# Fetching and converting two early feed-forward weights at other steps of an attention loop

## The chip, the core and the metric

The kernel runs on one core of a Trainium2 chip. The metric is the device time of one execution in microseconds (us), start to end. TensorE (PE; its weight loads are listed as PEld), VectorE (DVE), ScalarE (ACT), GpSimd (POOL) and SyncE (SP) each take their own instructions in order; transfers are issued from a queue of SP, ACT or POOL and run on 16 DMA engines.

## The reference

Attention with a mixing of heads before and after the softmax, then two feed-forward blocks one after the other:

```python
scores = scale * np.matmul(q, k.transpose(0, 1, 3, 2))      # 2 x 12 heads x 448 x 448
scores = np.einsum('bhij,hg->bgij', scores, w_pre)
attn = softmax(scores)                                      # over j, with 1e-9 added to the sum
attn = np.einsum('bgij,gh->bhij', attn, w_post)
x = np.matmul(attn, v)                                      # as 896 x 768
x = (silu(x @ w_gate) * (x @ w_val)) @ w_out                # 768 -> 1536 -> 768
h = x @ w_in                                                # 768 -> 2048
out = (h * np.clip(h + 3, 0, 6) / 6) @ w_out2               # 2048 -> 768
```

The feed-forward weights arrive as 64-bit floats. Each is brought to 32 bits on the chip by one ACT and four DVE operations (`convert_w`), and then split into a high and a low part, since each product is made of three matmuls.

## The kernel before

The 896 rows of queries are cut into eight tiles of about 112, each with ten or so chunks; two chunks make one step. There are 45 steps (0 to 44), which a Python loop writes out in full (L617 to L663), with LOOK = 2 steps of look-ahead. In step i the program writes, in this order:

- `exps(i+1)` (L261): ACT's exponentials of the next step;
- `av` and `av_rest` (L318, L337): products of finished weights of an earlier tile with v, and `postmix(i)` (L287), 56 small matmuls that mix heads after the softmax;
- `attn_out(i)` (L306): DVE and ACT each copy one PSUM bank of `postmix` out; `weights(i+1)` (L269 to L273): DVE's reciprocals and scaled mixing weights `wn`;
- `premix(i+2)` (L239) and `row_max(i+2)` (L252): the mixing before the softmax and DVE's row maxima `nm`;
- `qk` (L171): scores of a later tile, copied to the SBUF tile S one step on by DVE and ACT (L187);
- `relayout` (L204): up to three transfers from S into `sx` on SP's queue, which `premix` reads later, the first of them behind this step's `postmix`; `relayout_rest` (L220) does the remaining rows on POOL's queue;
- at the step's end ("end"), whatever the table put there: loads of q, k and v, `fetch` (L479) and `convert` (L490).

From step 36 on all tiles are scored, so steps have no `qk` and are shorter.

The table works as follows. `fetch(j, "early")` issues a third of weight j (two of six 128-row blocks, 256 KB of 64-bit words, tile `rg` for the gate weight, j = 0, and `rv` for the value weight, j = 1) on SP's queue. `convert(j, part)` issues the next one or two of 15 conversion operations; every group of four steps handles one third: ACT's Abs together with DVE's clamp, then a shift, and two merges (L414 to L419). The early raw tile has one buffer, so the first fetch of weight 1 comes after the last conversion of weight 0. `halve` (L497) splits the two finished weights at steps 42 and 43, and their first products run between the last steps of attention. The rest of the program, from about 185 us on, is feed-forward work.

In the transfers' names `q` is a tile's queries, `sx` the relaid scores, and in the trace's groups a buffer's number is left out.

Of the kernel before, what the change touches and what calls it, by code (L numbers as in the profile page):

```python
# [48 lines left out]
def kernel(  # L49
# [493 lines left out]
    def at_step(i, f, *args, place="end"):  # L543
        extra[i][place].append((f, args))
# [50 lines left out]
        at_step(scored[4 * b + 3] + 1, new_x, b)  # L595
    loads = [(0, load_v, 0, 2), (1, load_v, 0, 3), (4, load_q, 3), (6, load_q, 4)]
    loads += [(7 + n, load_k, 1, n, n + 1) for n in range(HP)]
    loads += [(15, load_q, 5), (21, load_q, 6), (27, load_q, 7)]
    loads += [(20 + 2 * j, load_v, 1, j) for j in range(JC)]
    loads += [(n, fetch, 0, "early") for n in (14, 17, 19)] + [(n, fetch, 1, "early") for n in (30, 32, 34)]  # L600
    for i, *load in loads:
        at_step(i, *load)

    for j in range(2):
        for n in range(12):
            at_step(17 + 14 * j + n, convert, j, 2 if n % 4 == 0 else 1)

    fillers = None

# [216 lines left out]
```

## Time and profile before

| what | us |
|---|---|
| median of 3 runs | 676.01 |
| lowest, highest | 674.33, 677.24 |
| the profiled execution | 674.53 |
| its span, first to last instruction | 672.7 |
| PE busy in it | 660.0 |

All numbers of the trace come from the one profiled execution, which lies 1.48 us below the median. Where a step is named by its time, it runs from the row maximum (L252) of the step before to its own. The granted TensorE clock is 1.00 in all windows listed.

### The profile page before, as it was taken

To read this page: it belongs to the slowest core of one execution; us is meant where nothing else is said; L and a number is where in the kernel's file an instruction comes from. 1 tells how busy PE (TensorE), PEld (TensorE's weight loads), DVE (VectorE), ACT (ScalarE), POOL (GpSimd) and SP (SyncE) were. 2 spreads that over 40 slices of the span, in tenths; PEclk is the share of its full clock that TensorE was granted. 3 is DMA by queue.
4 is the path that set the end of the run, shared out by engine and by line. 5 is a ranking of instruction groups with operands and counts; after the bars stand their busy time and mean duration, and the time that the engine had idled before them with its cause. 6 is when DMAs were issued, how large, how long until landed. Compare 5 with 4: busy or idle time off the path is not lost.

```text
span 672.7 us, 16147 instructions
## 1 busy us (share of the span) xinstructions
PE 660.0 (98%) x6685; PEld 561.9 (84%) x6685; DVE 500.1 (74%) x836; ACT 296.8 (44%) x603; POOL 160.5 (24%) x204
## 2 busy tenths in 40 slices
PE   9899999899999999999999999999999999999997
PEld 3456666566899999999999999999999999999997
DVE  4877889789278888888787666668888888756550
ACT  4766777677243434343442323245444553332220
POOL 3543366545202111311111000013333332000000
PEclk9999999999999999999999999999999999999999
DMA  7776576445022323223242333313222333544420
GB/s 245 228 217 190 175 219 200 156 148 205 3 95 95 134 100 138 98 104 131 98 137 95 99 136 101 133 67 121 95 95 95 102 117 92 165 140 149 151 67 27
DMA packets 34937, 86.87 MB, mean 129 GB/s; under 512 B 10064, under 2 KB 22752, under 8 KB 34864
## 3 DMA queue, kind: packets, MB, share of 16 engines
q1 hardware_dynamic: 26208, 81.14, 36.5%
q0 software_dynamic: 7936, 3.94, 2.4%
q8 instruction: 52, 0.85, 0.5%
q10 hardware_dynamic: 720, 0.76, 0.3%
q14 instruction: 21, 0.17, 0.1%
HBM read 62.37 MB, written 2.75 MB: 97 GB/s over the span
## 4 chain that ended last, share of the span: by engine, by line
PE 76%; DVE 17%; ACT 3%; DMA 2%; issue 1%; SPq 0%; ACTq 0%
PE pp L441 15%; PE po L441 13%; PE pv L441 12%; PE pg L441 12%; DVE yi L490 9%; PE pqk L171 5%; PE ppost L287 5%; PE pav L318 5%; PE ppre L239 5%; DVE rl L714 2%; PE p L441 2%; PE pav L337 2%; DVE yp L490 2%; DVE li L432 2%; ACT hi L427 2%; DMA q<-in_q_dram 1%
## 5 line engine op out<-in xcount | busy, mean ns | idle before, releaser
L441 PE MATMUL pp<-g,hp 128*128 128x448 f32 x384 | 108.3, 363 | 0.0
L690 POOL TENSOR_TENSOR g<-rl,g 128x448 fp32r<-128x448 f32 x32 | 41.3, 1309 | 167.8 <-ACT g L689 167.8
L441 PE MATMUL po<-u,ho 128*128 128x448 f32 x288 | 80.7, 361 | 0.0
L441 PEld LDWEIGHTS pp<-g,hp 128*128 128x128 f32 x384 | 72.0, 188 | 4.8
L261 ACT ACTIVATE e<-ppre,nm 128x448 f32<-128x448 f32 x90 | 56.3, 631 | 32.6 <-DVE nm L252 32.5
L441 PE MATMUL pi<-x2h,li 128*128 128x448 f32 x192 | 69.7, 363 | 0.0
L441 PE MATMUL pi<-x2l,hi 128*128 128x448 f32 x192 | 69.6, 362 | 0.0
L441 PE MATMUL pp<-g,lp 128*128 128x448 f32 x192 | 69.3, 361 | 0.2 <-DVE lp L432 0.2
L441 PE MATMUL pi<-x2h,hi 128*128 128x448 f32 x192 | 69.1, 360 | 0.0
L690 POOL TENSOR_TENSOR u<-sg,u 128x448 fp32r<-128x448 f32 x24 | 32.6, 1377 | 149.6 <-ACT u L689 149.6
L220 POOL DMA_DIRECT2D sx<-S x90 | 52.4, 583 | 50.8 <-issue 16.4
L441 PEld LDWEIGHTS po<-u,ho 128*128 128x128 f32 x288 | 54.0, 187 | 4.1
L287 PE MATMUL ppost<-wn,e 60*64 60x60 f32 x2520 | 51.3, 220 | 4.9 <-DVE wn L273 2.6
L252 DVE TENSOR_REDUCE nm<-ppre 128x1 f32<-128x448 f32 x90 | 51.8, 617 | 4.6 <-PE ppre L239 1.9
L441 PE MATMUL po<-u,lo 128*128 128x448 f32 x144 | 52.3, 363 | 0.0
L287 PEld LDWEIGHTS ppost<-wn,e 60*64 60x64 f32 x2520 | 45.2, 134 | 8.2 <-ACT at L306 3.0
L318 PEld LDWEIGHTS pav<-at,v 128*64 128x64 f32 x576 | 28.0, 136 | 28.7 <-ACT xs L360 15.7
L171 PE MATMUL pqk<-k,q 64*64 64x448 f32 (+3 forms) x384 | 48.1, 540 | 1.7 <-DMA q<-in_q_dram 1.4
L441 PE MATMUL pg<-xh,lg 128*128 128x448 f32 x132 | 47.9, 363 | 0.0
L441 PE MATMUL pv<-xh,lv 128*128 128x448 f32 x132 | 47.9, 363 | 0.0
L441 PE MATMUL pv<-xl,hv 128*128 128x448 f32 x132 | 47.8, 362 | 0.0
L441 PE MATMUL pg<-xl,hg 128*128 128x448 f32 x132 | 47.8, 362 | 0.0
(98 smaller groups left out, 1401.0 us busy)
## 6 DMA issues: line engine op xcount, KB each, us to landing
sx<-S SPq DMA_DIRECT2D x90, 182.0 KB
ri<-in_moe_w_in_dram SPq DMA_DIRECT2D x16, 768.0 KB
ro<-in_moe_w_out_dram SPq DMA_DIRECT2D x12, 768.0 KB
rg<-in_moe_w_gate_dram SPq DMA_DIRECT2D x11, 768.0 KB
rv<-in_moe_w_val_dram SPq DMA_DIRECT2D x11, 768.0 KB
rp<-in_moe_w_out_dram SPq DMA_DIRECT2D x12, 640.0 KB
rp<-in_moe_w_out_dram SPq DMA_DIRECT2D x6, 768.0 KB
sx<-S POOLq DMA_DIRECT2D x90, 42.0 KB, 4.7
```

The lines of the kernel that those rows point to most:

```text
L171: nc.tensor.matmul(p[e][lo:hi, :S], lhsT=qs[t][r, base + lo : base + hi], rhs=ks[b][r, c, :], start=True, stop=True, tile_position=(64 * e ...
L220: nc.gpsimd.dma_start(out=sx[m // 2][104:128, m % 2, :], in_=rows)
L239: nc.tensor.matmul(p[a][64 * r : 64 * r + 64, :S], lhsT=W1[rows, :], rhs=x[rows, r, :], start=True, stop=True, tile_position=(64 * a, 64 * r),
L252: top = nc.vector.tensor_reduce(nm[:, a : a + 1], pre[i][a][:, :S], AX.X, ALU.max, negate=True)
L261: nc.scalar.activation(e2[a], p[a][:, :S], AF.Exp, bias=nm[:, a : a + 1], scale=1.0, accum_out=sm[:, a : a + 1])
L287: mm = nc.tensor.matmul(p[s][64 * c : 64 * c + 64, at, :, :], lhsT=e2[a][rows, 64 * k : 64 * k + 64], rhs=wn[rows, a, :].rearrange("p (g k ...
L318: nc.tensor.matmul(p[64 * e : 64 * e + 64, : 2 * n], lhsT=vs[b][:, jc, h, :], rhs=ats[t][:, 2 * jc : 2 * jc + 2, h, :n], start=jc == 0, st ...
L337: mm = nc.tensor.matmul(pavs[t, c][64 * e : 64 * e + 64, a * n : a * n + n], lhsT=vs[b][rows, JC - 1, h, :], rhs=ats[t][rows, KB - 1, h, : ...
L427: nc.scalar.copy(hi_flat, y)
L441: nc.tensor.matmul(p[:, :S], lhsT=wt[:, kk, :], rhs=xx, start=start, stop=stop)
L490: f(*args)
L690: eng.tensor_tensor(to[1], src, to[0].bitcast(F32), ALU.subtract)
```

## The change

Three lines of the table are changed. The fetches of weight 0 go from the ends of steps 14, 17 and 19 to those of 13, 14 and 16, those of weight 1 from 30, 32 and 34 to 27, 29 and 31. The conversions of weight 0 go from steps 17 to 28 to steps 15 to 26, those of weight 1 from 31 to 42 to 28 to 39. The load of the last tile's q goes from the end of step 27 to that of step 28. It is read first by `qk` in step 30.

```diff
-    loads += [(15, load_q, 5), (21, load_q, 6), (27, load_q, 7)]
+    loads += [(15, load_q, 5), (21, load_q, 6), (28, load_q, 7)]
     loads += [(20 + 2 * j, load_v, 1, j) for j in range(JC)]
-    loads += [(n, fetch, 0, "early") for n in (14, 17, 19)] + [(n, fetch, 1, "early") for n in (30, 32, 34)]
+    loads += [(n, fetch, 0, "early") for n in (13, 14, 16)] + [(n, fetch, 1, "early") for n in (27, 29, 31)]
...
     for j in range(2):
         for n in range(12):
-            at_step(17 + 14 * j + n, convert, j, 2 if n % 4 == 0 else 1)
+            at_step(15 + 13 * j + n, convert, j, 2 if n % 4 == 0 else 1)
```

No instruction is added or dropped, and PE's and POOL's orders are the same. On SP's queue, around the ends of steps 27 to 31 (`S_119` and `S_120` are the two score tiles), there stands before:

```order
L204 DMA sx_2404<-S_120 104x1x448
L111 DMA q_2407<-in_q_dram 128x708
L204 DMA sx_2404<-S_120 104x1x448
L204 DMA sx_2485<-S_120 104x1x448
L204 DMA sx_2485<-S_119 104x1x448
L479 DMA rv_0_2633<-in_moe_w_val_dram 128x256
L204 DMA sx_2635<-S_119 104x1x448 x2
```

and after:

```order
L204 DMA sx_2406<-S_120 104x1x448
L479 DMA rv_0_2409<-in_moe_w_val_dram 128x256
L204 DMA sx_2406<-S_120 104x1x448
L204 DMA sx_2486<-S_120 104x1x448
L111 DMA q_2488<-in_q_dram 128x708
L479 DMA rv_0_2409<-in_moe_w_val_dram 128x256
L204 DMA sx_2486<-S_119 104x1x448
L204 DMA sx_2641<-S_119 104x1x448 x2
```

The first third of `rv` stands where q stood; q and the second third stand ahead of the transfer from `S_119`, where nothing but relayouts stood.

On ACT, at the end of step 28 (`xs` is the copy that closes it, the two `e` are the exponentials of step 29), there stands before:

```order
L306 COPY at_2467<-ppost_1_2430 128x84x5
L360 COPY xs_2072<-pav_5_2419 128x108
L261 ACTIVATE e_123,sm_2489<-ppre_0_2470,nm_2476 128x448
L261 ACTIVATE e_124,sm_2489<-ppre_1_2471,nm_2476 128x448
L187 COPY S_119<-pqk_4_1_2480 119x448
```

and after:

```order
L306 COPY at_2468<-ppost_1_2431 128x84x5
L360 COPY xs_2074<-pav_5_2420 128x108
L490 ACTIVATE yv_0_2490<-rv_0_2409 128x256
L261 ACTIVATE e_123,sm_2494<-ppre_0_2471,nm_2477 128x448
L261 ACTIVATE e_124,sm_2494<-ppre_1_2472,nm_2477 128x448
L187 COPY S_119<-pqk_4_1_2481 119x448
```

The first Abs of the value weight now stands ahead of the exponentials written in step 29.

On DVE, in steps 40 and 41, there stands before:

```order
L252 TENSOR_REDUCE nm_3376<-ppre_1_3371 128x1
L490 TENSOR_SCALAR yv_0_2715<-yv_0_2715 128x256
L348 MEMSET turns 1x1
L306 COPY at_3361<-ppost_0_3393 128x84x5
L269 TENSOR_SCALAR rc_3427<-sm_3380 128x2
L270 RECIPROCAL rc_3427<-rc_3427 128x2
L273 TENSOR_TENSOR wn_3430<-W_110,rc_3427 128x120
L382 TENSOR_TENSOR xl_3095<-pav_0_3383,xh_3094 128x110
L252 TENSOR_REDUCE nm_3440<-ppre_0_3434 128x1
L252 TENSOR_REDUCE nm_3440<-ppre_1_3435 128x1
L490 SCALAR_TENSOR_TENSOR yv_0_2715<-rv_0_2633,yv_0_2715 128x256
```

and after:

```order
L252 TENSOR_REDUCE nm_3379<-ppre_1_3374 128x1
L348 MEMSET turns 1x1
L306 COPY at_3364<-ppost_0_3395 128x84x5
L269 TENSOR_SCALAR rc_3429<-sm_3382 128x2
L270 RECIPROCAL rc_3429<-rc_3429 128x2
L273 TENSOR_TENSOR wn_3432<-W_110,rc_3429 128x120
L382 TENSOR_TENSOR xl_3098<-pav_0_3385,xh_3097 128x110
L252 TENSOR_REDUCE nm_3442<-ppre_0_3436 128x1
```

Both conversions there are gone; they stand three steps earlier.

## Rows read from the trace of the kernel before

**Rows 1.** The page: PE's busy time, and the queue of instruction transfers (packets, MB, share).

```profile
PE 660.0 (98%) x6685; PEld 561.9 (84%) x6685; DVE 500.1 (74%) x836; ACT 296.8 (44%) x603; POOL 160.5 (24%) x204
...
q8 instruction: 52, 0.85, 0.5%
```

**Rows 2.** Waits, 16 to 170 us: waiter <- releaser: us in total, times, longest us.

```profile
PE ppost L287 <- issue: 2.4, 3, 1.8
...
PE pav L337 <- DVE turns L348: 1.2, 3, 0.4
```

**Rows 3.** Windows of single steps: us, each engine's busy us (x instructions), PEclk, DMA share, GB/s.

```profile
76.79:80.19 3.40, 3.40 (x96) 2.14 (x92) 2.87 (x9) 2.55 (x8) 1.06 (x2) 1.00 0.71 225
80.19:84.20 4.01, 3.60 (x96) 2.42 (x92) 3.10 (x9) 2.71 (x8) 1.21 (x3) 1.00 0.10 28
91.07:94.46 3.39, 3.39 (x96) 2.14 (x92) 3.14 (x9) 2.54 (x8) 2.61 (x5) 1.00 0.80 232
94.46:98.23 3.77, 3.62 (x96) 2.47 (x92) 3.10 (x10) 2.70 (x8) 2.71 (x6) 1.00 0.84 249
...
118.39:123.86 5.47, 3.67 (x96) 2.43 (x92) 3.23 (x9) 2.45 (x8) 1.87 (x4) 1.00 0.58 179
...
148.05:150.74 2.69, 2.69 (x84) 1.71 (x82) 2.44 (x10) 1.90 (x6) 2.12 (x4) 1.00 0.38 124
...
162.83:165.87 3.04, 2.64 (x82) 1.66 (x80) 2.97 (x10) 2.06 (x7) 1.43 (x2) 1.00 0.77 279
```

**Rows 4.** Windows from the start to each of PE's three waits for issue.

```profile
0.00:82.80 82.80, 77.03 (x1738) 42.27 (x1739) 62.35 (x165) 53.66 (x143) 35.24 (x66) 1.00 0.70 214
0.00:97.00 97.00, 91.10 (x2120) 51.34 (x2120) 74.79 (x201) 63.88 (x172) 45.88 (x84) 1.00 0.69 211
0.00:121.50 121.50, 114.78 (x2755) 66.34 (x2755) 96.77 (x264) 81.47 (x222) 59.56 (x107) 1.00 0.69 211
```

**Rows 5.** Timeline of step 29: start us, us, engine, instruction [idle before <- releaser].

```profile
118.15 0.25 ACT L360 COPY xs<-pav 128x108 f32<-128x108 f32 x1
...
119.11 0.64 ACT L261 ACTIVATE e<-ppre,nm 128x448 f32<-128x448 f32 x1 [0.71 <-DVE nm L252]
...
122.63 0.38 PE L287 MATMUL ppost<-wn,e 60*64 60x60 f32 x9 [1.80 <-issue]
...
123.04 0.52 ACT L306 COPY at<-ppost 128x420 f32<-128x420 f32 x1 [2.17 <-PE ppost L287]
```

**Rows 6.** Timeline of SP's queue around the load of the last q.

```profile
115.28 1.25 SPq L111 DMA_DIRECT2D q<-in_q_dram  x1
116.65 10.61 SPq L204 DMA_DIRECT2D sx<-S  x3
127.30 0.45 SPq L479 DMA_DIRECT2D rv<-in_moe_w_val_dram  x1
```

**Rows 7.** Timeline: the first Abs of the value weight.

```profile
130.81 0.44 ACT L490 ACTIVATE yv<-rv 128x256 f32<-128x256 f32 x1 [0.25 <-DMA rv<-in_moe_w_val_dram]
```

**Rows 8.** The chain that ended last, 15 to 185 us: the q of another tile.

```profile
33.28 8.56 DMA q<-in_q_dram
```

**Rows 9.** The three relayouts that POOL issued from 116.0 to 119.5 us.

```profile
DMA to landing us min/median/max: 6.4/6.8/7.9
```

**Rows 10.** Timeline of steps 41 and 42.

```profile
163.89 0.77 DVE L490 SCALAR_TENSOR_TENSOR yv<-rv,yv 128x256 uint32<-128x256 uint32 x1
...
164.74 0.27 PE L337 MATMUL pav<-at,v 64*64 64x55 f32 x2 [0.40 <-DVE turns L348]
...
167.99 0.32 PE L337 MATMUL pav<-at,v 64*64 64x55 f32 x4 [0.36 <-DVE turns L348]
```

**Rows 11.** Timeline of SP's queue, 60 to 92 us.

```profile
64.39 5.67 SPq L204 DMA_DIRECT2D sx<-S  x6
70.11 0.97 SPq L479 DMA_DIRECT2D rg<-in_moe_w_gate_dram  x1
...
87.69 0.47 SPq L479 DMA_DIRECT2D rg<-in_moe_w_gate_dram  x1
```

## The prediction, made before the changed kernel ran

> **What bounds the kernel now.** The page comes first: PE is busy for 660.0 of 672.7 us [rows 1], so whatever the change is worth must show as PE standing still, or as PE's work starting later. Everything that moves lies between 65 and 170 us, in the attention loop; behind it the feed-forward part follows at once, so a microsecond gained or lost in the loop is one at the end. The second view is windows of single steps [rows 3]. A step with scores takes 3.39 to 3.40 us, and PE is busy for all of it, with a conversion in it (DVE 3.14 us busy) or without (2.87). So in a long step a conversion costs nothing: DVE has some 0.3 us left. Three long steps are longer: 4.01 us from 80.19, 3.77 from 94.46, and 5.47 from 118.39. Against 3.40 these are 0.61, 0.37 and 2.07 us, 3.05 together. A short step takes 2.69 us at best and 3.04 in the window from 162.83, where DVE is busy for 2.97.
>
> The third view, the waits, names the causes: PE waits three times, 2.4 us in all, for "issue" in front of `postmix`, and three times, 1.2 us, for DVE's `turns` [rows 2]. The first kind needs a reading. PE has started 3477, 4240 and 5510 matmuls and weight loads when it stops [rows 4]; between the stops lie 763 and 1270. Instructions are brought in 52 packets of together 0.85 MB [rows 1], 16.3 KB each, and PE's 13,370 matmuls and weight loads over 52 are 257. 763 is 3.0 times that, 1270 is 4.9 times (register and semaphore instructions are not counted). So I read these stops as PE at the end of a block of instructions whose successor has not come: the block travels on the same DMA engines, and in the steps ahead of the first two stops they are busy at 0.71 and 0.80 [rows 3].
>
> The Trainium skill, "Runtime: NRT & Kernel Launch", section "Instruction fetch mechanics", says that instructions are refilled in 16 KiB blocks, fetched while the one before is executed, and that crossing a boundary is mostly hidden. The size agrees with the row; "mostly" leaves out a stop of 1.8 us. By that rule alone a stop would not follow the load on the DMA engines; that is rival four.
>
> **Part one: conversions leave the last steps.** Before, weight 1 is converted up to step 42; after, up to 39. Two of PE's three waits for `turns` stand right behind a conversion of the short steps: 0.40 us behind a merge of 0.77 us, and 0.36 us [rows 10]. These conversions go: a gain of 0.76 us. In turn the end of step 39 now has a merge where a clamp or shift stood, and the step behind may wait the 0.40 us that such a merge costs. Bounds -0.76 and -0.36; I take **-0.5**, as the step behind step 39 also has slack in the longer work on PE. The conversions that arrive in steps 15, 16 and 28 to 30 are hidden by PE's 3.39 us.
>
> **Part two: the third fetch of weight 0 leaves 87.69 us.** In its place nothing goes, and all three fetches shift up SP's queue: a new one between the relayouts that follow 64.39, then those at 70.11 and at the place of the second [rows 11]. 256 KB are 262,144 bytes; at the best rate of a window, 249 GB/s [rows 3], a fetch takes 1.05 us of all engines. Ahead of the stop at 97 us there is a fetch less: the 0.37 us may go. Bounds -0.37 and 0; I take **-0.3**. Ahead of the stop at 82.8 us there is one more, still queued if the engines have not caught up in ten microseconds; then the block comes up to 1.05 us later. They run empty in the step of the stop (share 0.10), but only there, so I take half, **+0.5**, with bounds 0 and +1.05. The first Abs of weight 0 has some six microseconds from the new fetch to step 15's end; it is not late by the bounds below unless the worst holds.
>
> **Part three: around 118 us.** Here lies the main term. SP issues q at 115.28 [rows 6]; after, the first fetch of weight 1 stands at this place, and ACT wants it at the end of step 28, when its copy ends at 118.40 [rows 5]. That leaves 3.12 us. How long does it take? From below: the same fetch, issued at 127.30 behind a long gap, ended ACT's wait at 130.81, so 3.51 us [rows 6, 7]. From above: another tile's q, some 360 KB and also issued two steps ahead, took 8.56 us [rows 8]. Near in time and load, POOL's relayouts issued at 116.0 to 119.5 took 6.4 to 7.9, median 6.8 [rows 9]. I take 6.8: the data come at 122.1, and ACT stands for 3.7 us with the next step's exponentials behind it (bounds 0.4 and 5.4). What hides it? ACT had 0.71 us of waiting for DVE before those exponentials and 2.17 us before its copy of `postmix`, while PE stood at the block's end [rows 5]: 2.88 us. DVE stands too, since its clamp waits for the Abs and the S copy, `wn` and `nm` wait behind it. So the wait costs 3.7 - 2.9 = **+0.8** us, bounds 0 and +2.5. The 1.80 us stop would hold the cover; with it gone, the wait itself is late next and takes its place. The block's way is a little freer (256 KB for 354 KB ahead of it), so the stop itself may shrink: this is worth something only if the data come early, down to -1.8.
>
> q of the last tile now goes out after the two relayouts of 116.65 [rows 6], near 118.9, and `qk` reads it in step 30. By 6.8 us it is there at 125.7, by 8.56 at 127.5, and step 30's scores come three microseconds behind the row maximum at 123.86, near 126.7 or later. So q costs 0 to 0.8 us; taken as nothing, since ACT's wait puts `qk` later. With the second fetch it loads the engines where they had run empty; PE's next block boundary, 257 instructions on, may become a stop. Its bounds are 0 and +1.8 (the largest stop seen, in a like crowd); I take **+0.2**. The third fetch near 130 us replaces two later ones: 0.
>
> **The sum.** -0.5 - 0.3 + 0.5 + 0.8 + 0.2 = +0.7 us, on the profiled 674.53: 675.2. That execution lies 1.48 us under the median, so against the runs I say 676.01 + 0.7 = **676.7 us**.
>
> **The rivals.**
> 1. *The stop goes, nothing takes its place.* The fetch lands as fast as in rows 7, in 3.5 us, and with less queued ahead of the block PE's 1.80 us stop falls away, with the 0.37 and the 0.76 us: -2.9, 673.1 us. For it: q was the largest transfer in that stretch. Against: the fetch of rows 7 found empty engines, this one does not. Chance 0.2.
> 2. *The new wait on ACT decides, slower.* The fetch takes 8.56 us and lands at 123.84; ACT stands for 5.4 us, 2.5 beyond the cover; with the 82.8 us stop at +1.05, a new block stop of 1.8, and part one at -0.5, it is +4.85: 680.9 us. From a landing later than 121.3 (118.40 + 2.9) every microsecond counts in full. For it: POOL's 7.9 us. Against: it is 256 KB, not 360. Chance 0.12.
> 3. *The table changes nothing that matters.* PE's order is the same and all moves stay under cover but for part one and the 0.3: -0.8, 675.2 us. It lies inside the forecast's range and shares its chance.
> 4. *Stops are bound to the place in the program, not to the DMA load.* Then the second part and the new block stop are 0, and -0.5 + 0.8 = +0.3 remains: 676.3 us. For it: they fall on whole blocks. Against: other blocks end without a stop. Chance 0.1. The page of the skill named above would have it so.
>
> **How the numbers follow.** Forecast (with rival 3) 0.58, rival 1 0.2, rival 2 0.12, rival 4 0.1. 0.5% of 676.01 is 3.4 us, about what a measurement of this kernel can tell from no change; the shown runs alone lie 2.9 us apart. All gains that rows name, 3.05 + 0.76 = 3.8 us, barely exceed it: faster by more than 0.5%, 0.04. Slower by more: most of rival 2 and the end of the forecast's range, 0.11. Within: 0.85. The range reaches down to 673.5, which takes half of rival 1, and up to 679.3, which leaves out most of rival 2; outside stay about 0.2.
>
> **What would show it.** Right: an Abs of `yv` on ACT near 122 us with an idle time of 3 to 4 us before it that a DMA of `rv` ended; the step from 118.4 us at 5.5 to 6.3 us; no wait for `turns` in the last two steps of the loop; the 97 us stop gone and the one at 82.8 longer. Wrong: that step under 4 us (rival 1); a wait of PE for q in step 30; a stop of PE for issue at a place where none was; all three stops unchanged (rival 4). A change by more than 1 us behind 185 us would be no part of this reasoning.

## The result and the profile after

The changed kernel took 680.38 us in the median of 12 runs (674.49 to 684.34), the kernel before 675.87 us (12 runs, 673.56 to 677.92): a ratio of 1.0065 with an interval of 1.0044 to 1.0086, so it is slower by 4.5 us. The forecast was 676.7, with a range up to 679.3. The profiled execution of the changed kernel took 679.84 us (span 678.1) against 674.53 (span 672.7) before.

First the page of the changed kernel: PE's busy time, and the granted clock in 40 slices of 17 us. PE is busy for 3.1 us more than in [rows 1] with the same 6685 matmuls, so part of the loss is work that takes longer, beside PE standing still. The eighth slice, 119 to 136 us, shows where: its clock is 7 tenths, while before all slices stood at 9.

```profile
PE 663.1 (98%) x6685; PEld 564.1 (83%) x6685; DVE 499.5 (74%) x836; ACT 296.4 (44%) x603; POOL 160.8 (24%) x204
...
PEclk9999999799999999999999999999999999999999
```

The windows of single steps answer to [rows 3]: us, each engine's busy us (x instructions), PEclk, DMA share, GB/s. They are steps 18, 22, 29 and 30.

```profile
79.71:84.33 4.62, 3.61 (x96) 2.42 (x92) 3.24 (x9) 2.49 (x7) 1.62 (x4) 1.00 0.16 48
94.59:98.37 3.78, 3.61 (x96) 2.47 (x92) 3.24 (x9) 2.44 (x7) 2.71 (x6) 1.00 0.85 247
118.76:126.22 7.46, 4.72 (x96) 3.02 (x92) 3.11 (x10) 2.66 (x9) 1.60 (x4) 0.81 0.71 197
126.22:131.59 5.37, 5.37 (x98) 3.21 (x94) 3.19 (x9) 2.50 (x7) 1.06 (x2) 0.63 0.01 2
```

Step 29 took 7.46 us for 5.47 before, and step 30 took 5.37 us for 3.41 (123.86 to 127.27 in the trace of before). Those two steps hold 3.95 of the 5.4 us by which the span grew. In step 30 PE waits for nothing at all: it is busy for 5.37 of 5.37 us, at a mean clock of 0.63. Step 18 grew by 0.61 us and step 22 by 0.01.

The last steps of the loop are better compared over the same work of PE than from row maximum to row maximum, where PE is not always equally far. These windows run from the start of PE's 3674th matmul to that of its 4002nd and on to that of its 4084th, first the two stretches of before and then the same two of after:

```profile
156.65:168.24 11.59, 10.83 (x330) 7.71 (x328) 10.67 (x32) 8.36 (x24) 5.94 (x9) 1.00 0.58 206
168.24:171.54 3.30, 3.30 (x87) 2.73 (x83) 1.25 (x6) 1.10 (x3) 2.61 (x4) 1.00 0.00 2
...
161.28:172.63 11.35, 10.82 (x331) 7.58 (x329) 8.93 (x29) 7.40 (x22) 5.57 (x9) 1.00 0.58 206
172.63:176.53 3.90, 3.51 (x86) 2.86 (x82) 1.37 (x6) 1.90 (x5) 2.69 (x4) 1.00 0.04 15
```

The first stretch is 0.24 us shorter after the change, the second 0.60 us longer.

The chain of waits, in order of time, tells how step 29 ends (start, us, what):

```profile
115.46 7.52 DMA rv<-in_moe_w_val_dram
...
123.76 0.53 DVE S L187
124.29 0.04 DVE turns L348
```

The first third of the value weight is issued at 115.46, lands 7.5 us later, and between it and PE stand ACT's Abs, DVE's clamp, DVE's copy of `S` and the small memset of `turns`. The timeline of the same stretch gives each engine's wait in brackets; `q` is the last tile's, issued behind the weight (compare [rows 5, 6]):

```profile
118.91 1.58 SPq L111 DMA_DIRECT2D q<-in_q_dram  x1
...
121.72 0.44 PE L287 MATMUL ppost<-wn,e 60*64 60x60 f32 x10 [0.52 <-issue]
...
123.00 0.43 ACT L490 ACTIVATE yv<-rv 128x256 f32<-128x256 f32 x1 [4.23 <-DMA rv<-in_moe_w_val_dram]
...
123.47 0.29 DVE L490 TENSOR_SCALAR yv<-yv 128x256 f32<-128x256 f32 x1 [3.55 <-ACT yv L490]
...
124.37 0.36 PE L337 MATMUL pav<-at,v 64*64 64x60 f32 x2 [2.21 <-DVE turns L348]
```

ACT stood for 4.23 us, DVE for 3.55 us behind it, and PE for 2.21 us, since the small memset of `turns` that releases it is queued on DVE behind the clamp and the copy of `S`. The block stop of PE that was to cover the wait, 1.80 us before, is 0.52 us here.

Two more windows cut steps 29 and 30 at the clock's change instead of at the steps:

```profile
118.76:123.40 4.64, 2.88 (x80) 1.80 (x72) 1.16 (x2) 0.41 (x3) 1.15 (x3) 1.00 0.85 231
123.40:130.20 6.80, 5.83 (x71) 3.49 (x74) 4.37 (x15) 4.02 (x13) 0.45 (x1) 0.50 0.21 61
```

PE began to stand still at about 122.2, and from 123.4 on its granted clock is 0.50, the 1.2 GHz level, for 6.8 us. PE is busy for 5.83 us of these. The eight matmuls of `qk` took 1.91 us at this level (at 125.94) and 0.96 in the next step (at 131.35, clock 1.00), half as long. If all of the 5.83 us would halve, the clock costs some 2.9 us (an estimate from these rows). The rest of the 3.95 us, 1.0, is about what PE stands still for longer: 0.52 + 2.21 = 2.73 us where it was 1.80.

The remaining places are PE's two stops for issue in steps 41 and 42 and a wait at 175.5, in the timeline (against [rows 10]):

```profile
165.47 0.32 PE L337 MATMUL pav<-at,v 64*64 64x55 f32 x3 [0.25 <-issue]
...
169.30 0.46 PE L287 MATMUL ppost<-wn,e 60*64 60x60 f32 x17 [0.25 <-issue]
...
175.46 0.76 PE L287 MATMUL ppost<-wn,e 60*64 60x60 f32 x37 [0.39 <-DVE turns L348]
```

and the windows from the start to four of PE's stops for issue (for the first two see [rows 4]; the first two brackets count the matmuls and the weight loads):

```profile
0.00:82.90 82.90, 76.23 (x1738) 42.46 (x1739) 62.74 (x167) 53.63 (x143) 35.58 (x67) 1.00 0.72 217
0.00:121.50 121.50, 114.21 (x2755) 66.53 (x2755) 95.46 (x259) 79.63 (x217) 59.28 (x106) 1.00 0.70 211
0.00:165.30 165.30, 155.03 (x3770) 92.63 (x3770) 130.62 (x363) 108.05 (x300) 79.66 (x140) 0.98 0.63 192
0.00:169.20 169.20, 158.62 (x3896) 95.24 (x3897) 133.60 (x372) 110.51 (x307) 80.72 (x142) 0.98 0.62 189
```

The first two come at the same counts as before (1738 and 1739; 2755 and 2755), but they last differently: 1.01 us where [rows 3] gave 0.41 of PE standing, and 0.52 where it was 1.80.

### The profile page after: what moved, and what is told of

Read it like the earlier page. It is cut to its first block, busy times and chain, and to the rows that moved or that the text cites. A ratio compares the mean times of both kernels' runs of the same rounds, so it can differ in the third digit from the quotient of the medians.

```text
span 678.1 us, 16147 instructions
## 1 busy us (share of the span) xinstructions
PE 663.1 (98%) x6685; PEld 564.1 (83%) x6685; DVE 499.5 (74%) x836; ACT 296.4 (44%) x603; POOL 160.8 (24%) x204
## 4 chain that ended last, share of the span: by engine, by line
PE 94%; DMA 3%; DVE 1%; ACT 1%; issue 1%; SPq 0%
PE pi L441 17%; PE pp L441 17%; PE po L441 13%; PE pg L441 12%; PE pv L441 12%; PE pqk L171 5%; PE ppost L287 5%; PE ppre L239 5%; PE pav L318 5%; PE pav L337 2%; PE p L441 2%; DMA q<-in_q_dram 1%; DMA rv<-in_moe_w_val_dram 1%; DMA k<-in_k_dram 1%; ACT e L261 0%
## 5 line engine op out<-in xcount | busy, mean ns | idle before, releaser
L239 PE MATMUL ppre<-sx,W 64*64 64x448 f32 x360 | 48.4, 553 | 0.0
```

What stands on the lines that cost most here:

```text
L239: nc.tensor.matmul(p[a][64 * r : 64 * r + 64, :S], lhsT=W1[rows, :], rhs=x[rows, r, :], start=True, stop=True, tile_position=(64 * a, 64 * r),
```

## The experiments

Theory A: the loss comes from the first conversion of weight 1, which stands at the end of step 28 and reaches ACT before its data do. The wait stops ACT, DVE and at last PE, and PE's clock then falls. Theory B, the main rival: the moved transfers crowd the DMA engines, so that instruction blocks, `q` and relayouts come late wherever one looks. A third possibility is that the late stops in steps 40 to 42, or weight 0's part, carry the loss. In the diffs, "after" or "before" tells which kernel was edited.

**The conversion alone put back (late_conv).** Edit of after: the fetches stay early, the conversions of weight 1 begin two steps later, at step 30.

```diff
-            at_step(15 + 13 * j + n, convert, j, 2 if n % 4 == 0 else 1)
+            at_step(15 + 15 * j + n, convert, j, 2 if n % 4 == 0 else 1)
```

> The changed kernel with only the conversions of weight 1 two steps later (steps 30 to 41 for 28 to 39); all fetches and q stay at the changed places. Theory A (the loss is ACT waiting for the first fetch of weight 1: 4.2 us in the changed kernel's trace, PE standing behind it and then working at the lower of its two clocks for 6.8 us): the data have landed by step 30, so no wait of ACT for rv, granted clock 1.000, steps from 118 to 131 us back to 3.4 and at most 5.5 us, about 676 us, within 1 us of the kernel before. Theory B (the loss is the crowd on the DMA engines, q and two fetches within 5 us, which holds up PE's instructions): time stays near 680 us, with waits of PE for issue in steps 29 and 30.

Measured: 676.89 us against 675.77 before, a ratio of 1.001 (0.9986 to 1.0033). The transfers are those of after, and the loss is gone: A, not B. (The last conversions are back at steps 40 and 41 too, so this kernel takes back much of part one as well; conv29 below moves them by one step only.) In the trace (timeline, then windows of steps 29 and 30) the weight's third has 8.6 us and ACT no longer waits for it; steps 29 and 30 are at 3.39 us and full clock.

```profile
119.46 0.47 SPq L479 DMA_DIRECT2D rv<-in_moe_w_val_dram  x1
121.99 1.02 SPq L111 DMA_DIRECT2D q<-in_q_dram  x1
...
128.03 0.45 ACT L490 ACTIVATE yv<-rv 128x256 f32<-128x256 f32 x1
129.82 0.97 PE L171 MATMUL pqk<-k,q 64*64 64x448 f32 x8 [1.65 <-DMA q<-in_q_dram]
```

```profile
121.42:124.81 3.39, 3.39 (x96) 2.13 (x92) 2.86 (x8) 2.44 (x8) 1.90 (x4) 1.00 0.88 240
124.81:128.20 3.39, 3.37 (x92) 1.78 (x84) 2.88 (x8) 2.54 (x8) 0.46 (x1) 1.00 0.77 212
```

Now PE waits 1.65 us for the last tile's `q`, 7.8 us after its issue. That goes with `q` being loaded one step later, behind a weight's third. In after this wait does not show; there step 29 ends 1.4 us later than here (126.22 against 124.81), so its data had come.

**One step instead of two (conv29).** Edit of after, as above with `15 + 14 * j + n`: the conversions begin at step 29.

> The changed kernel with the conversions of weight 1 one step later (29 to 40 for 28 to 39). ACT then wants the first fetch 6.5 us after its issue, and in two executions so far the fetch took 7.5 us. Theory A (ACT's wait and the clock behind it): ACT waits about 1 us, of which its usual 0.7 us in front of the exponentials hides most; no PE wait over 0.5 us, clock mostly full, 675.5 to 677.5 us, between the 30 to 41 variant and the kernel before. Theory B (the crowd): 679 us or more.

Measured: 675.9 us against 674.67, ratio 1.0006 (0.9981 to 1.0031). One step is enough, though not without a trace (timeline): the third is still late, by 1.11 us, and `q` by 1.04.

```profile
123.91 0.45 ACT L490 ACTIVATE yv<-rv 128x256 f32<-128x256 f32 x1 [1.11 <-DMA rv<-in_moe_w_val_dram]
...
127.43 0.97 PE L171 MATMUL pqk<-k,q 64*64 64x448 f32 x8 [1.04 <-DMA q<-in_q_dram]
```

The conversions at step 28, 29 and 30 with the same transfers give +0.65%, +0.06% and +0.1%, where only the first interval excludes zero.

**The wait without the crowd (early_conv).** Edit of before: no transfer moves; the conversions of weight 1 begin one step earlier, so that the first Abs is just as unready.

```diff
-            at_step(17 + 14 * j + n, convert, j, 2 if n % 4 == 0 else 1)
+            at_step((17 if j == 0 else 30) + n, convert, j, 2 if n % 4 == 0 else 1)
```

> The kernel before with only the conversions of weight 1 one step earlier (30 to 41 for 31 to 42). The first Abs then stands in the very step at whose end its data are fetched, and nothing else moves: no q, no second fetch, DMA engines empty before. Theory A (ACT's wait for the fetch is the loss): the fetch takes 3.5 us as before, ACT stands about 3 us with DVE and PE behind it, PE idles 1.5 to 2.5 us in step 30 or 31 and may then drop to its lower clock: 677.5 to 680 us. Theory B (the crowd on the DMA engines is the loss): no crowd here, so 675.8 us as before.

Measured: 681.48 us (6 runs, 677.64 to 687.13) against 675.44, ratio 1.0108 (1.0058 to 1.0158). The wait alone makes the kernel slower. Timeline and the window of step 31:

```profile
127.06 0.45 SPq L479 DMA_DIRECT2D rv<-in_moe_w_val_dram  x1
130.46 0.43 ACT L490 ACTIVATE yv<-rv 128x256 f32<-128x256 f32 x1 [3.49 <-DMA rv<-in_moe_w_val_dram]
132.78 0.27 PE L337 MATMUL pav<-at,v 64*64 64x60 f32 x2 [3.19 <-DVE turns L348]
```

```profile
127.02:133.83 6.81, 3.62 (x96) 2.42 (x92) 3.12 (x9) 2.76 (x8) 3.10 (x6) 1.00 0.52 171
```

The third lands 3.4 us after its issue, as fast as in [rows 7], and 3.49 us of wait on ACT become 3.19 us on PE, for there is no block stop in this step. This execution kept the full clock through the wait and took 677.64 us, 2.2 us over before's median. The other five ran at a mean clock of 0.990 to 0.997 and took 679.7 to 687.1 us.

**`q` back ahead of the weight (q_back).** Edit of after: the third lands later still.

```diff
-    loads += [(15, load_q, 5), (21, load_q, 6), (28, load_q, 7)]
+    loads += [(15, load_q, 5), (21, load_q, 6), (27, load_q, 7)]
```

> The changed kernel with only q moved back to step 27, where it stands ahead of the first fetch of weight 1 on SP's queue. Theory A: the fetch is issued 1.3 us later and comes behind 354 KB more, so ACT waits 1 to 2.5 us longer than its 4.2 us: 681 to 683 us. Theory B: the crowd after 118 us is less by a q, so that 677 to 679 us result.

Measured: 682.83 us (6 runs) against 675.77, ratio 1.0104 (1.0069 to 1.0138). In the trace ACT waits 2.35 us longer than in after. The loss comes out larger too, as A has it, though its interval overlaps that of after. Timeline and windows of step 29, of step 30 and of the stretch at the lower clock:

```profile
127.62 0.43 ACT L490 ACTIVATE yv<-rv 128x256 f32<-128x256 f32 x1 [6.58 <-DMA rv<-in_moe_w_val_dram]
128.99 0.36 PE L337 MATMUL pav<-at,v 64*64 64x60 f32 x2 [5.39 <-DVE turns L348]
```

```profile
121.03:130.83 9.80, 4.41 (x96) 2.83 (x92) 3.10 (x9) 2.66 (x9) 1.26 (x3) 0.79 0.59 164
130.83:135.62 4.79, 4.79 (x98) 2.76 (x94) 3.19 (x9) 2.49 (x7) 0.76 (x1) 0.73 0.00 0
126.60:133.40 6.80, 4.41 (x30) 2.38 (x32) 3.93 (x11) 4.41 (x13) 0.45 (x1) 0.50 0.14 47
```

**PE kept at work during the wait (after_busy).** Edit of after: 40 matmuls of zeros, 80 columns each, in PE's order of step 29, into a part of the bank that nobody reads. The lines of this kernel are shifted by 10.

```diff
+    def busy29():
+        for n in range(40):
+            nc.tensor.matmul(banks29[1][:, 420:500], lhsT=idle[:, :128], rhs=idle[:, :80], start=True, stop=True)
```

> The changed kernel with 40 additional matmuls of zeros (bf16, 80 columns, into unused columns of a bank) in step 29 behind the mixing after the softmax, where PE stood for 2.2 us. They add 2 to 3 us of PE work where PE waits for DVE anyway, and change no wait of ACT. If the lower clock after the wait is a cost of its own (theory A with the clock): the granted clock stays 1.000, step 30 takes 3.4 to 4 us in place of 5.4, and the time falls by 1.5 to 3 us to 677.5 to 679 us, nearer to the runs of the changed kernel whose clock was 1.000. If the wait alone counts: about 680 us or more.

Measured: 682.07 us (10 runs) against 675.44, ratio 1.008 (1.0049 to 1.0112); the expected time is missed. Windows of step 30 and of a later stretch, then the timeline:

```profile
125.93:129.12 3.19, 3.19 (x94) 2.10 (x92) 2.92 (x11) 2.39 (x7) 0.43 (x2) 1.00 0.04 13
...
171.20:175.00 3.80, 3.80 (x30) 2.98 (x31) 1.30 (x5) 1.44 (x3) 1.56 (x2) 0.50 0.02 4
```

```profile
123.13 0.43 ACT L500 ACTIVATE yv<-rv 128x256 f32<-128x256 f32 x1 [4.52 <-DMA rv<-in_moe_w_val_dram]
124.49 0.27 PE L347 MATMUL pav<-at,v 64*64 64x60 f32 x2 [1.79 <-DVE turns L358]
...
171.19 0.58 PE L297 MATMUL ppost<-wn,e 60*64 60x60 f32 x12 [2.50 <-issue]
```

In this execution ACT waits as in after, yet PE's clock stays at 1.00 and step 30 takes 3.19 us for 5.37. PE also stands for less, 1.79 us where it was 2.73, since the added matmuls fill part of the wait and the block stop is absent. In exchange a block stop of 2.50 us ends at 171.2, and the clock falls there. So the local effect is seen once, and no gain shows in the runs. As a measure of what the clock costs over all runs the experiment is inconclusive; it also adds 80 instructions.

**Weight 0's part alone (w0_only).** Edit of before: fetches at (13, 14, 16) and conversions from step 15, only for weight 0.

```diff
-            at_step(17 + 14 * j + n, convert, j, 2 if n % 4 == 0 else 1)
+            at_step((15 if j == 0 else 31) + n, convert, j, 2 if n % 4 == 0 else 1)
```

> The kernel before with only weight 0 moved (fetches at 13, 14, 16; conversions from step 15). Theory A: only the stop of PE near 82.8 us grows, from 0.4 to 1.0 us as in the changed kernel's trace: 676.5 us, clock 1.000. Theory B gives weight 0 a larger share of the 4.5 us lost: 677.5 us or more.

Measured: 675.43 us against 675.77, ratio 0.9995 (0.9973 to 1.0016). This part costs and gives nothing that the runs can tell. In its trace the stop at 82.8 us is absent, and others stand in its place (timeline). The clock falls in this trace too, behind a wait for another tile's `q`: it is 0.50 from 45.0 to 48.0 us.

```profile
44.69 1.53 PE L171 MATMUL pqk<-k,q 64*64 64x448 f32 x8 [2.05 <-DMA q<-in_q_dram]
...
100.72 0.26 PE L287 MATMUL ppost<-wn,e 60*64 60x60 f32 x1 [0.66 <-issue]
...
107.73 0.26 PE L337 MATMUL pav<-at,v 64*64 64x55 f32 x2 [0.88 <-issue]
```

**The last tile's `q` alone (q_only).** Edit of before: `load_q, 7` at step 28 for 27.

> The kernel before with only the load of the last q moved from step 27 to step 28. Theory A: q makes no loss of its own. It is issued near 119 us in place of 115.3 us, and with it gone from ahead of the block that PE waits for at 121 us, the stop of 1.8 us there shrinks to 0.5 us as in the changed kernel: about 674.6 us, if q lands before step 30 reads it. Theory B: the stop moves on to the next block or a wait for q takes its place: 676 us or more.

Measured: 675.62 us against 675.77, ratio 1.0004 (0.9979 to 1.0029). No gain. With `q` gone from ahead of it the block stop is still 1.61 us, at the same count, and another has come up later (timeline, and the window from the start):

```profile
122.14 0.38 PE L287 MATMUL ppost<-wn,e 60*64 60x60 f32 x9 [1.61 <-issue]
...
161.10 0.32 PE L337 MATMUL pav<-at,v 64*64 64x55 f32 x3 [1.14 <-issue]
```

```profile
0.00:121.50 121.50, 115.48 (x2755) 65.85 (x2755) 96.72 (x264) 81.40 (x222) 59.77 (x107) 1.00 0.69 212
```

**Looking for a faster kernel (mid, q3_early, mid_q3).** mid takes weight 0's part, the fetches of weight 1 at (28, 30, 32) and its conversions from step 30 (edit of before). q3_early loads another tile's `q`, that of [rows 8], two steps earlier. mid_q3 is both.

```diff
-    loads = [(0, load_v, 0, 2), (1, load_v, 0, 3), (4, load_q, 3), (6, load_q, 4)]
+    loads = [(0, load_v, 0, 2), (1, load_v, 0, 3), (2, load_q, 3), (6, load_q, 4)]
```

> Weight 0 as in the changed kernel; weight 1 fetched at steps 28, 30 and 32 and converted at 30 to 41; q at step 27 as before. The first fetch has two steps before its Abs. Theory A: no wait of ACT for rv and none of PE for q, 675.0 to 676.0 us. Theory B (the fetch ahead of the tile change is itself the trouble): 677 us or more.

> The kernel before with the q of the fourth tile loaded at step 2 in place of step 4. All traces so far show PE waiting 1.4 to 2.1 us for it near 42 us. If that wait is a loss by itself: 1 to 2 us faster than the kernel before, about 674.3 us. If the transfer only pushes aside the relayouts beside it: no gain or a loss, 675.5 to 678 us.

> Weight 0 as in the changed kernel, weight 1 fetched at 28, 30, 32 and converted at 30 to 41, q of the last tile at 27, and q of the fourth tile at step 2. It leaves out both the wait of ACT for rv and the long wait of PE for a q near 42 us. If the waits add up: 673.5 to 675 us, faster than both kernels. If the stops of PE at block ends take the place of each wait that goes: 675 to 676 us.

Measured: mid 675.03 against 675.44, ratio 0.9992 (0.9965 to 1.0019); q3_early 675.45, ratio 0.9993 (0.9968 to 1.0019); mid_q3 675.94 against 674.67, ratio 1.0008 (0.9983 to 1.0032). None beats the kernel before. mid's first third is 1.45 us late on ACT, and PE stands for 1.15 us (timeline); the runs show no loss from it.

```profile
128.80 0.45 ACT L490 ACTIVATE yv<-rv 128x256 f32<-128x256 f32 x1 [1.45 <-DMA rv<-in_moe_w_val_dram]
...
131.13 0.27 PE L337 MATMUL pav<-at,v 64*64 64x60 f32 x2 [1.15 <-DVE turns L348]
```

q3_early removes the wait that it aims at, and its waits over 16 to 175 us then list stops for issue, six of them in front of `postmix` alone, where before had three with 2.4 us [rows 2]:

```profile
PE ppost L287 <- issue: 5.3, 6, 2.1
```

## Why the prediction was wrong

**What was right.** The place and the mechanism. An Abs of `yv` on ACT near 122 us (123.00), ended by a DMA of `rv`, after an idle time that the prediction put at 3 to 4 us (4.23); DVE's clamp and copy behind it; PE released by `turns`. It is rival 2's mechanism, with a landing later than the 121.3 us from which that rival decides. The forecast took a landing 6.8 us after the issue, from POOL's relayouts [rows 9]; the trace shows 7.54. That row was a better guess than the fetch on empty engines [rows 7], and the error of 0.7 us is small. late_conv and early_conv show from both sides that this wait makes the loss, and that the crowd without it does not.

**The step that failed is part three's price: the sum had no term for PE's clock.** +0.8 us was the price of PE standing still, and PE did stand still for 0.93 us longer (2.73 for 1.80). But 6.8 us at the 1.2 GHz level followed, some 2.9 us by the rows above, which is more than half of the profiled difference of 5.3. So steps 29 and 30 together grew by 3.95 us where the sum had 0.8. The trace of before could not have shown it in this place: its clock was 1.00 in every window, behind a stop of 1.80 us too. How often it happens shows over the runs. Of the 12 runs of after, two had a mean clock of 0.999 or more (674.49 and 677.28 us); of the 79 runs of before that stood beside the experiments, 51 had. The four kernels whose weight is late for ACT (after, q_back, early_conv, after_busy) had 6 of 34, the other seven 58 of 84. after's mean clock, 0.9958, is 0.27% under the 0.9985 of those 79 runs (the 12 runs of before that stand beside the result have no clock on record). Taken in proportion, that is 1.8 of the 4.5 us (an estimate). How the 4.5 us of the medians divide is therefore known only roughly: 1.8 us of clock by this, more than half by the one profiled pair. The rest would be PE standing still, but only one execution's waits were seen, and no experiment took the clock away alone: after_busy, meant for that, did not get faster. That the late weight makes the loss is shown; the clock's share of it stays open.

**The cover.** 2.17 of the 2.88 us set against the wait lay under a block stop of 1.80 us. This stop is no fixed part of the kernel: in the traces it is 1.80 in before, 2.08 in q3_early, 1.61 in q_only, 0.52 in after, and absent in w0_only and late_conv. The prediction saw that the cover depended on it and still took it whole. In early_conv, where no stop stands in the step, 3.49 us on ACT cost 3.19 on PE: that is the price without cover.

**Part one: half the gain, and it did not last.** Expected -0.5. The two waits for `turns` that [rows 10] shows, 0.76 us together, are gone, as foretold, and the step behind step 39 has no new one. But two stops of 0.25 us for issue stand there instead, and over the same matmuls 0.24 us is gained. Behind it 0.60 us is lost, 0.39 of them in the wait at 175.46, so the two stretches together are 0.36 us longer. That wait is put down to `turns`, but PE has 4023 matmuls and 4023 weight loads behind it there and its weight loads stand for issue for 0.49 us: it may be a block's end. No experiment took this part alone, so this is a reading of one pair.

**Part two: one half right.** The stop at 82.8 us is 0.6 us longer, by the +0.5 of the forecast; the one at 97 us did not go (step 22 at 3.78 for 3.77), where -0.3 was expected. w0_only shows the whole part at 0.9995, so the runs do not tell whether either term is real.

**`q` of the last tile.** No wait for it in after, but 1.65 us in late_conv and 1.04 in conv29: "taken as nothing, since ACT's wait puts `qk` later" held, with its bound of 0.8 too low for the kernels in which ACT's wait goes. The +0.2 for PE's next block boundary is not seen: step 31 took 3.40 us.

**Rival 1** fell: the stop can go, as in late_conv and w0_only, and the total does not follow. **Rival 4** is half right. The stops come at fixed counts, 2755 and 2755 in before, after, q_only and q3_early. after_busy tells a place in the program from a block's end. It has 80 more matmuls and weight loads ahead of its stop at 171.2, and the total there, 8047, is one block on from a stop of after:

```profile
0.00:170.50 170.50, 160.56 (x4023) 96.15 (x4024) 135.80 (x380) 113.78 (x317) 82.99 (x144) 1.00 0.63 196
```

That is 254 more than the 7793 (3896 and 3897) at which after stops at 169.30, and 7793 is 253 more than its 7540 (3770 and 3770, at 165.47), where q_only stops too, at 161.10. The prediction's 257 was 3 or 4 too large. So the count of instructions, in blocks of 253 or 254, decides where a stop can come. Which block's end has one, and how long it is, differs from trace to trace; with one trace of each kernel the part of the transfers cannot be told from chance. By the Trainium skill, "Runtime: NRT & Kernel Launch", section "Instruction fetch mechanics", crossing such a boundary is mostly hidden; the traces agree for most of the some 31 boundaries up to there (8047 over 254), and the 2.50 us above are an exception.

**The chances.** 0.12 for rival 2 was too low. It was priced by the landing alone, 8.56 us, as if the kernel had to be that late for such a loss. Here a landing after 7.5 us came with 4.5 us.

## What to carry to other kernels

When a conversion and its fetch are moved together, the time between issue and first use has to be read for the new place in the queue: 3.4 us on empty engines became 7.5 us behind other transfers here, and one more step of lead was worth the whole loss. An in-order engine that stands for late data can cost twice when the bound engine stands behind it, once by standing and once by the clock that the bound engine gets back with; a sum with a PE wait like the one here should carry a term for that. A cover that is itself a stop found in one execution should not be taken whole. Small stops that were removed came back elsewhere here: seven kernels moved them without a change of time that the runs could tell.

## What the runs showed of the hardware

PE's granted clock fell to its 1.2 GHz level while PE stood still for 2.21 us (after), 5.39 us (q_back) and 2.50 us (after_busy, at 171.2), and behind stops of 1.99 us (conv29, at 35.0) and 2.05 us (w0_only, at 44.7). It stayed at 2.4 GHz through 3.19 us (early_conv), 2.08 us (q3_early, at 123.8) and 1.80 us (before). So the length of the stop alone did not decide in these executions. Once down it stayed so for 6.8 us in after and in q_back. In late_conv it fell behind a stop of PE for issue of 2.46 us that ended at 36.4, for about 3.5 us (window):

```profile
37.50:41.00 3.50, 3.50 (x56) 1.93 (x52) 1.78 (x4) 1.77 (x5) 0.69 (x2) 0.51 0.64 203
```

The kernel before has such executions too: 28 of 79 had a mean clock under 0.999. A median of this kernel is therefore a mixture, and a change can move it by making the lower clock more frequent, which the profile of one execution cannot foretell.
